# One zero fill of a decode kernel split anew over the 16 DMA engines: 39 small transfers in place of six

## The chip, the cores and the metric

One Trainium2 chip, one of its cores. The metric is the device time of one execution in microseconds (us). Before: a median of 779.5 us over three runs (779.49 to 779.59). In this text "engine" with a number, 0 to 15, is one of the core's 16 DMA engines; TensorE, VectorE (DVE), ScalarE (ACT), GpSimd (POOL) and SyncE (SP) are called by their names.

## The reference

One decode step of a transformer block and its gradients. Sizes: model width D = 448, 16 query heads on 8 key/value heads of width 256, a cache of 32768 positions of which only the last W = 4096 are attended to, a gated feed-forward of width 1792. The core of it:

```python
k = jnp.repeat(k_cache[:, :, Sk - W:, :], rep, axis=1)
v = jnp.repeat(v_cache[:, :, Sk - W:, :], rep, axis=1)
...
h = x + _A_ref(_layernorm(x, axis=-1), A_k_cache, A_v_cache, A_wq, A_wo)
h2 = h + _B_ref(_layernorm(h, axis=-1), B_w_gate, B_w_up, B_w_down)
...
_out, _vjp = jax.vjp(_f, A_x, A_k_cache, A_v_cache, A_wq, A_wo, B_w_gate, B_w_up, B_w_down)
```

The outputs are h2 and the gradients of the eight inputs. The gradients of the two caches (out_2 and out_3) have the caches' full size, 8 x 32768 x 256 in bf16 each. Outside the last 4096 positions they are zero. So for each of the 8 heads and each of the two outputs a region of 28672 x 256 zeros, 14336 KB, has to be written: 16 regions, 224 MB, of the 280.59 MB that the kernel writes in all.

## The kernel before, in words

Computation and zero fills run side by side. The computation loads the last 4096 positions of K and V head by head, makes scores, softmax and the moments that the backward pass needs (L339 to L397), goes through the feed-forward both ways, and in a second loop over the heads (L696) forms the gradients of K and V and stores them through ScalarE's queue (L739). GpSimd forms and stores the weight gradients from about 440 us on. Nothing in the computation reads a fill; the only tie at the end is `fills_done` (L284), where VectorE waits for all fills before it writes one element (L287).

**The fills.** A region is seen as 896 rows of 16384 bytes (ZW = 8192 bf16). The source is a tile of SBUF whose every fourth partition holds zeros: 32 partitions, each read 28 times by a stride of 0 (`rows_of`, L240). One transfer of 896 rows is spread by the chip over all 16 engines, 56 rows each. The first two regions come from the tile `pair` with rows of 32768 bytes (L252). The other 14 come from `home` (`Z_late`), in `fill_late` (L258 to L282), all on SyncE's queue (ZQ). The loop keeps two fills under way: before it issues fill i it waits (L265) until fill i-2 has landed, counted in `zsem[0]` or `zsem[1]`, to which each transfer adds 16. The scheduler moves these waits into the issuing instructions.

**The uneven fill.** One region, number UNEVEN = 3 (the second of the 14), is not spread evenly. Only its first 704 rows go out as one transfer, 44 rows an engine. The other 192 go out as six small transfers, each from a few partitions, so that an engine gets as many rows as the list in L272 says. Each entry is (partitions, first partition, rows from each, queue):

```python
for e, base, rows, queue in ((3, 0, 8, nc.gpsimd), (2, 12, 2, nc.gpsimd), (3, 20, 13, nc.gpsimd), (8, 64, 13, nc.gpsimd), (4, 0, 5, ZQ), (1, 0, 1, ZQ)):
```

A transfer from e partitions runs on e engines. GpSimd's four cover 3 + 2 + 3 + 8 = 16 engines once, with 8, 2, 13 and 13 rows; SyncE's two start again at the first engine, with 5 rows on engines 0 to 3 and one more on engine 0. Counted by engine, 0 gets 8 + 5 + 1 = 14 extra rows, 1 and 2 get 13, 3 gets 2 + 5 = 7, 4 gets 2, and 5 to 15 get 13 each. GpSimd's transfers count in `psem` (64 in all), SyncE's in `zsem[1]`, so that the fill after next waits for SyncE's two as well.

**Order around it.** GpSimd issues its four directly behind the loads of two V tiles (L207), at 131.4 us, and its next instruction is a load of half a K tile (L418) that waits until 235 us. SyncE issues its two between the first late fill and the 704 rows; behind the last fill it has only the waits that end the program (L793).

Of the kernel before, what the change touches and what calls it, by code (L numbers as in the profile page):

```python
# [27 lines left out]
ZW = 16 * KB  # L28
# [7 lines left out]
def kernel(  # L36
        ctx, tc, A_x, A_k_cache, A_v_cache, A_wq, A_wo, B_x, B_w_gate, B_w_up, B_w_down, grad_out,
           out_0, out_1, out_2, out_3, out_4, out_5, out_6, out_7, out_8):
    nc = tc.nc
    LD = nc.scalar  # L40
    ZQ = nc.sync
# [29 lines left out]
    Z_late = home[:]  # L71
# [134 lines left out]
    def load_kv(dst, cache, g, queue=LD):  # L206
        queue.dma_start(out=dst, in_=cache[0, g, Sk - W:, :].rearrange("(p t) d -> p t d", t=T))  # L207
# [32 lines left out]
    def rows_of(src, n):  # L240
        return src[0:128:4].unsqueeze(1).to_broadcast([32, n, src.shape[1]])

    def fill_with(dst, src, sem, group, queue=ZQ):
        fill = queue.dma_start(out=dst, in_=src)
        tc.info.no_tile_sem_insts.add(fill.ins.name)
        tc.add_to_no_dep_group(group, fill.ins)
        tc.keep_in_program_order(fill.then_inc(sem, 16))
# [7 lines left out]
    for g in (5, 6):  # L255
        load_kv(V_of[g], A_v_cache, g, nc.gpsimd)

    def fill_late():  # L258
        zsem = [tc.alloc_semaphore(f"zsem{j}") for j in range(DEEP)]
        psem = tc.alloc_semaphore("psem")  # L260
        due = [0] * DEEP
        for i, reg in enumerate(regions[EARLY:]):
            j = i % DEEP
            if i >= DEEP:
                tc.keep_in_program_order(ZQ.wait_ge(zsem[j], due[j]))  # L265
            n = NZ
            if i + EARLY == UNEVEN:
                odd = reg.rearrange("(r f) -> r f", f=ZW)[22 * 32:]
                reg = reg[0:22 * 32 * ZW]
                n = 22  # L270
                at = 0
                for e, base, rows, queue in ((3, 0, 8, nc.gpsimd), (2, 12, 2, nc.gpsimd), (3, 20, 13, nc.gpsimd), (8, 64, 13, nc.gpsimd), (4, 0, 5, ZQ), (1, 0, 1, ZQ)):  # L272
                    fill_with(odd[at:at + e * rows].rearrange("(e n) f -> e n f", e=e),
                              Z_late[base:base + 4 * e:4].unsqueeze(1).to_broadcast([e, rows, ZW]), zsem[j] if queue is ZQ else psem, "fills", queue)
                    at += e * rows
                    if queue is ZQ:
                        due[j] += 16
            for dst, src in [(reg.rearrange("(p n f) -> p n f", p=32, f=ZW), rows_of(Z_late, n))]:
                fill_with(dst, src, zsem[j], "fills")
                due[j] += 16  # L280
        return zsem, psem, due

    def fills_done(zsem, psem, due):
        tc.keep_in_program_order(nc.vector.wait_ge(psem, 64))  # L284
        for j in range(DEEP):
            tc.keep_in_program_order(nc.vector.wait_ge(zsem[j], due[j]))
        filled = tc.keep_in_program_order(nc.vector.memset(done_t[:], 0.0))  # L287
        tc.declare_fence(filled.ins, group="fills")
# [43 lines left out]
    with tc.tile_pool(name="ps_x", bufs=1, space=bass.MemoryType.PSUM) as ps_x, \  # L332
# [72 lines left out]
        for g in range(G):  # L405
            p_f = p_next
            if g < G - 2:
                p_next = scores(g + 1)
            if g == 1:
                clear_rows()  # L410
                fill_sems = fill_late()
            moments(g, p_f)
            for w, h in NEXT.get(g, ()):
                load_kv((K_of, V_of)[w][h], (A_k_cache, A_v_cache)[w], h)
            if g == G - 4:
                LD.dma_start(out=K_of[G - 1][:, 0:T // 2, :], in_=k_last[:, 0:T // 2, :])
            if g == G - 2:
                nc.gpsimd.dma_start(out=K_of[G - 1][:, T // 2:, :], in_=k_last[:, T // 2:, :])  # L418
                p_next = scores(G - 1)
                LD.dma_start(out=wo_sb[:, JW:], in_=wo_v[:, JW:])  # L420
                LD.dma_start(out=dh_bc[0:1, :], in_=A_x.rearrange("a b d -> (a b) d"))
# [179 lines left out]
    with tc.tile_pool(name="work2", bufs=2) as work2, tc.tile_pool(name="lnw", bufs=1) as lnw, \  # L601
# [94 lines left out]
        for it, g in enumerate((6, 1, 3, 4, 5, 0, 7, 2)):  # L696
# [52 lines left out]
            if it == 6:  # L749
# [16 lines left out]
                nc.vector.tensor_copy(out=dx_bf[:, 384:D], in_=dx_ps[0:1, 384:D])  # L766
                LD.dma_start(out=out_1.rearrange("a b d -> (a b) d"), in_=dx_bf)
        fills_done(*fill_sems)

# [28 lines left out]
```

## Time and profile before

| | |
|---|---|
| median of three runs | 779.5 us |
| the profiled execution: its own time, its span | 779.39 us, 777.6 us |
| written to HBM, read from HBM | 280.59 MB, 49.38 MB |
| SyncE's queue q1, share of 16 engines' time | 75.4% |
| ScalarE's queue q10 | 16.1% |
| GpSimd's queue q0 | 8.0% |
| TensorE, VectorE busy | 58%, 49% |
| last compute instruction ends; last fill's completion | 746.9 us, 775.93 us |

The page has the span in 40 slices with the busy share of the DMA engines in tenths; the view of windows gives that share (1.00 is all 16 engines busy; overlaps of neighbouring packets make it up to 1.01) and the GB/s for any stretch; the waits name who was waited for; the issues name each transfer's queue, size and time to landing. Below them the trace keeps one record for each DMA packet, with queue, start, duration and size. A row of 16384 bytes is one packet, and a transfer's completion is a packet of 4 bytes on each engine.

### The profile page before, as it was taken

The numbers are of one execution on the slowest core, as the hardware profiler recorded it, in microseconds if no ns is written. First come the engines' busy times: TensorE is split into PE (matmuls) and PEld (weight loads), VectorE is DVE, ScalarE is ACT, GpSimd is POOL, SyncE is SP. The second block draws the span as 40 slices with busy tenths as digits, with TensorE's granted clock in tenths as the row PEclk, the third lists the DMA queues.
The fourth block names the chain that finished last, engine by engine and source line by source line (L and its number), as shares of the span: only waits on it lengthen the run. The fifth ranks groups of instructions, "written<-read, shape, count | busy, mean of one in ns | idle before, by whom it ended". The sixth has DMA issues, their size and how long they took to land.

```text
span 777.6 us, 6520 instructions
## 1 busy us (share of the span) xinstructions
PE 450.8 (58%) x2205; PEld 191.2 (25%) x2205; DVE 382.6 (49%) x1132; ACT 198.6 (26%) x309; POOL 196.5 (25%) x113
## 2 busy tenths in 40 slices
PE   1999999796993755231142898532108886830310
PEld 1444444342441322010021233210003332300100
DVE  8168656351570723332369428463104853679520
ACT  1442332334200100000001127332103733540220
POOL 7000001000000010020001157363293938196000
PEclk9999999898896776555555799755558965765555
DMA  9999999999999999999999999999999999999997
GB/s 378 429 422 423 433 438 417 429 429 427 429 430 430 429 430 429 431 431 428 429 432 432 430 429 430 431 429 431 432 432 429 429 429 430 431 429 428 432 431 300
DMA packets 23398, 330.40 MB, mean 425 GB/s; under 512 B 1920, under 2 KB 2181, under 8 KB 4645
## 3 DMA queue, kind: packets, MB, share of 16 engines
q1 hardware_dynamic: 14826, 250.43, 75.4%
q10 hardware_dynamic: 4266, 53.39, 16.1%
q0 software_dynamic: 4272, 26.17, 8.0%
q8 instruction: 17, 0.28, 0.1%
q14 instruction: 17, 0.13, 0.0%
HBM read 49.38 MB, written 280.59 MB: 424 GB/s over the span
## 4 chain that ended last, share of the span: by engine, by line
DVE 16%; PE 15%; DMA 14%; another core or an unknown queue 4%; ACT 2%; issue 1%; DVEq 0%; ACTq 0%
DMA out_dram<-arena 11%; PE d_ps L729 4%; PE rows_ps L322 4%; DVE pair L753 3%; PE tr_ps L319 3%; DVE arena L737 3%; DVE arena L736 3%; DVE arena L551 2%; PE dqb_ps L607 2%; DVE arena L704 1%; DMA arena<-in_B_w_up_dram 1%; PE dqb_ps L613 1%; DMA arena<-in_A_v_cache_dram 1%; ACT arena L734 1%
## 5 line engine op out<-in xcount | busy, mean ns | idle before, releaser
L381 DVE TENSOR_SCALAR arena<-arena,p_f 128x256 bf16<-128x256 bf16 x512 | 109.4, 281 | 29.9 <-PE M_t L385 29.9
L319 PE MATMUL tr_ps<-ident_f,arena 128*128 128x128 f32 x448 | 83.0, 316 | 63.1 <-DMA arena<-in_A_v_cache_dram 41.0
L322 PE MATMUL rows_ps<-arena,vpad 128*16 128x512 bf16 x256 | 87.8, 437 | 11.8 <-DVE arena L704 5.9
L338 ACT COPY arena<-tr_ps 128x1024 bf16<-128x1024 bf16 x64 | 63.5, 1013 | 109.0 <-PE tr_ps L319 105.0
L319 PEld LDWEIGHTS tr_ps<-ident_f,arena 128*128 128x128 f32 x448 | 55.3, 157 | 109.8 <-issue 60.5
L729 PE MATMUL d_ps<-arena 32*128 32x512 bf16 x256 | 48.3, 519 | 55.1 <-DVE arena L737 45.1
L385 PE MATMUL M_t<-arena 128*128 128x512 bf16 x320 | 78.7, 392 | 0.0
L736 DVE CAST arena<-d_ps 128x512 bf16<-128x512 f32 x64 | 44.1, 688 | 49.6 <-PE d_ps L729 48.9
L737 DVE CAST arena<-d_ps 128x512 bf16<-128x512 f32 x64 | 43.5, 680 | 20.9 <-DMA out_dram<-arena 20.9
L733 ACT CAST arena<-d_ps 128x512 bf16<-128x512 f32 x64 | 37.8, 590 | 62.0 <-PE d_ps L729 60.2
L702 ACT COPY arena<-tr_ps 128x1024 bf16<-128x1024 bf16 x32 | 32.6, 1020 | 76.2 <-PE tr_ps L319 57.1
L734 ACT CAST arena<-d_ps 128x512 bf16<-128x512 f32 x64 | 38.2, 596 | 20.5 <-DMA out_dram<-arena 20.5
L385 PEld LDWEIGHTS <-arena 128*128 128x128 bf16 x320 | 30.5, 101 | 38.5 <-issue 10.1
L505 PE MATMUL r_ps<-arena,X2pad 128*2 128x448 bf16 x24 | 10.3, 564 | 49.5 <-DMA arena<-in_B_w_gate_dram 39.1
L324 DVE COPY rows_t<-rows_ps 16x512 f32<-16x512 f32 x8 | 5.4, 679 | 63.4 <-PE rows_ps L322 63.3
L729 PEld LDWEIGHTS <-arena 32*128 32x128 bf16 x256 | 11.1, 96 | 94.1 <-DVE arena L737 60.2
L624 POOL TENSOR_SCALAR arena<-dh_bc,oX_f 128x448 bf16<-128x448 bf16 x18 | 25.1, 1402 | 27.9 <-DMA out_dram<-arena 27.8
L207 POOL DMA_DIRECT2D pair<-in_A_v_cache_dram x2 | 1.3, 632 | 114.7 <-POOLq L253 114.7
L436 POOL DMA_DIRECT2D arena<-in_B_w_gate_dram x4 | 3.1, 773 | 105.9 <-DVE dhn L495 64.5
L704 DVE COPY arena<-tr_ps 128x1024 bf16<-128x1024 bf16 x32 | 22.5, 704 | 14.7 <-PE tr_ps L319 13.4
L322 PEld LDWEIGHTS <-vpad 128*16 128x16 bf16 x256 | 17.4, 90 | 45.0 <-issue 41.0
L385 PE MATMUL M_t<-arena,pair 128*128 128x512 bf16 x128 | 28.0, 379 | 0.0
(257 smaller groups left out, 641.3 us busy)
## 6 DMA issues: line engine op xcount, KB each, us to landing
out_dram<-home SPq DMA_DIRECT2D x13, 14336.0 KB, 78.9
out_dram<-arena ACTq DMA_DIRECT2D x16, 2048.0 KB, 18.6
out_dram<-pair SPq DMA_DIRECT2D x2, 14336.0 KB, 93.6
out_dram<-home SPq DMA_DIRECT2D x1, 11264.0 KB
arena<-in_A_k_cache_dram ACTq DMA_DIRECT2D x4, 2048.0 KB, 20.7
arena<-in_A_k_cache_dram SPq DMA_DIRECT2D x3, 2048.0 KB, 19.6
arena<-in_A_v_cache_dram SPq DMA_DIRECT2D x3, 2048.0 KB
arena<-in_A_v_cache_dram ACTq DMA_DIRECT2D x3, 2048.0 KB, 32.8
```

The lines of the kernel that those rows point to most:

```text
L319: nc.tensor.transpose(tr_ps[:, i, :], X_sb[:, 4 * q + i, :].bitcast(f32), ident_f[:])
L322: nc.tensor.matmul(rows_ps[:], lhsT=pad[:, e, 16 * q:16 * q + 16], rhs=XT.rearrange("p (n e) -> p n e", e=2)[:, :, e], start=(q == 0 and e ...
L338: sT_ps = dots(K_of[g], KT_slot, vpad[g % 2], rows1, ps_c, "cols", lambda q, XT, ps: nc.scalar.copy(out=XT, in_=ps))
L381: nc.vector.tensor_scalar(out=pK[:, i, hh, :], in0=K_sb[:, t, :], scalar1=p_f[:, 8 * i + c, hh:hh + 1], scalar2=None, op0=ALU.mult)
L385: nc.tensor.matmul(M_ps[vh], lhsT=V_sb[:, t, vh * 128:(vh + 1) * 128], rhs=pK[:, i, :, :].rearrange("p h d -> p (h d)"), start=(t == 0), s ...
L702: nc.scalar.copy(out=XT, in_=ps)
L704: nc.vector.tensor_copy(out=XT, in_=ps)
L729: nc.tensor.matmul(d_ps[:, qi].rearrange("p w d -> p (w d)"), lhsT=rm[32 * q:32 * (q + 1), l, :], rhs=Rs[32 * q:32 * (q + 1), :], start=Tr ...
L733: nc.scalar.copy(out=stV[:, t:t + 2, :], in_=d_ps[:, :, 0, :])
L734: nc.scalar.copy(out=stK[:, t:t + 2, :], in_=d_ps[:, :, 1, :])
L736: nc.vector.tensor_copy(out=stV[:, t:t + 2, :], in_=d_ps[:, :, 0, :])
L737: nc.vector.tensor_copy(out=stK[:, t:t + 2, :], in_=d_ps[:, :, 1, :])
```

## The change

The same region is split anew. Its regular transfer shrinks from 704 to 480 rows, 30 an engine. The remaining 416 rows, 26 an engine, go out as 26 transfers on GpSimd's queue and 13 on SyncE's. GpSimd's come in pairs, for m from 2 to 14: one row each from the first m partitions, then two rows each from the other 16 - m. SyncE's 13 no longer stand at the uneven fill: they come behind the last of the 14 fills, one row each from the first k partitions, for k from 14 down to 2. All take the partitions 0, 4, 8 ... 60, where before the last eight were 64, 68 ... 92. `psem` now counts to 416, and the wait for the fill after next counts the 480 rows alone.

```diff
+    def fill_rows(rows, at, e0, k, n, sem, queue):
+        fill_with(rows[at:at + k * n].rearrange("(e n) f -> e n f", e=k),
+                  Z_late[4 * e0:4 * (e0 + k):4].unsqueeze(1).to_broadcast([k, n, ZW]), sem, "fills", queue)
...
-                odd = reg.rearrange("(r f) -> r f", f=ZW)[22 * 32:]
-                reg = reg[0:22 * 32 * ZW]
-                n = 22
+                n = 15
+                single = reg.rearrange("(r f) -> r f", f=ZW)[n * 32:]
+                reg = reg[0:n * 32 * ZW]
                 at = 0
-                for e, base, rows, queue in ((3, 0, 8, nc.gpsimd), (2, 12, 2, nc.gpsimd), (3, 20, 13, nc.gpsimd), (8, 64, 13, nc.gpsimd), (4, 0, 5, ZQ), (1, 0, 1, ZQ)):
-                    fill_with(odd[at:at + e * rows].rearrange("(e n) f -> e n f", e=e),
-                              Z_late[base:base + 4 * e:4].unsqueeze(1).to_broadcast([e, rows, ZW]), zsem[j] if queue is ZQ else psem, "fills", queue)
-                    at += e * rows
-                    if queue is ZQ:
-                        due[j] += 16
+                for m in range(2, 15):
+                    for e0, k, rows in ((0, m, 1), (m, 16 - m, 2)):
+                        fill_rows(single, at, e0, k, rows, psem, nc.gpsimd)
+                        at += k * rows
...
+        for k in range(14, 1, -1):
+            fill_rows(single, at, 0, k, 1, zsem[j], ZQ)
+            due[j] += 16
+            at += k
         return zsem, psem, due
...
-        tc.keep_in_program_order(nc.vector.wait_ge(psem, 64))
+        tc.keep_in_program_order(nc.vector.wait_ge(psem, 26 * 16))
```

Nothing else differs. The order of the instructions on TensorE, VectorE and ScalarE is the same.

## The prediction

> **What bounds the kernel now.** First the page's slices of the span, to see which resource never rests.
>
> ```profile
> DMA  9999999999999999999999999999999999999997
> ...
> q1 hardware_dynamic: 14826, 250.43, 75.4%
> q10 hardware_dynamic: 4266, 53.39, 16.1%
> q0 software_dynamic: 4272, 26.17, 8.0%
> ```
>
> The 16 DMA engines are busy in every slice but the last; the three queues' shares add up to 99.5%. TensorE has 58%. So the span is the DMA work, and the question is how evenly 16 engines finish it. The view of windows over the end (the last two columns are the DMA share and GB/s) shows that:
>
> ```profile
> 746.00:768.00 22.00, 0.00 (x0) 0.00 (x0) 0.88 (x2) 0.71 (x2) 0.00 (x0) 0.50 1.01 434
> 768.00:770.00 2.00, 0.00 (x0) 0.00 (x0) 0.00 (x0) 0.00 (x0) 0.00 (x0) 0.50 0.94 401
> 770.00:772.00 2.00, 0.00 (x0) 0.00 (x0) 0.00 (x0) 0.00 (x0) 0.00 (x0) 0.50 0.67 287
> 772.00:774.00 2.00, 0.00 (x0) 0.00 (x0) 0.00 (x0) 0.00 (x0) 0.00 (x0) 0.50 0.17 74
> 774.00:776.00 2.00, 0.00 (x0) 0.00 (x0) 0.00 (x0) 0.00 (x0) 0.00 (x0) 0.50 0.06 25
> ```
>
> All 16 work until 768; the share then falls as engines run out, to 0.06 = 1/16 from 774 to 776: one engine alone. Compute is over (746.9 us), and the waits (us in total, times, longest) say who waits for that engine, and SyncE's own waits who comes behind:
>
> ```profile
> DVE done_t L287 <- DMA out_dram<-home: 29.6, 1, 29.6
> ```
>
> ```profile
> SPq L793 <- DVE done_t L287: 15.3, 1, 15.3
> ```
>
> The last 16 completions (4-byte packets) of SyncE's queue lie at 768.0, 768.8, 769.6, 770.4, 770.9, 771.5, then seven from 772.1 to 772.6, 774.1, 774.4 and 775.93 us; their mean is 771.9. The span ends 1.67 us after the last, the execution's own time (779.39) 1.79 us after the span.
>
> **Which engine is last.** A packet record names no engine, but on a busy engine a packet starts 3 or 4 ns before its predecessor ends, so records sort into 16 trains. A row of 16384 bytes takes 611 ns, so one every 607 ns; of 15776 such packets after 60 us 14858 took just that. Of the longer ones 889 took up to 700 ns, 12 ns over on average, 10.4 us in all, most of it on one train; it has none while TensorE rests (700 to 720, after 748). I followed this slow train at two places. From 130 to 230 us its GpSimd packets are two V loads of 8 rows and then **2** rows, and its SyncE packets go from 56 rows to 44 with no small transfer between: by front's list this is engine 4, the only one with 2 and none. From 718 to the end no other train has its phase, and it ends at **775.93**. So engine 4 is last although it has 11 rows (6.7 us) less than engines 5 to 15. Engine 3 (2 rows, then 5 of SyncE) carries most of the 309-ns instruction packets of queue q14; where one was clear (at 150.8 us) the row behind it took 1244 ns in place of 611, 0.94 us in all.
>
> **The change part by part.**
>
> *Rows per engine.* Let T be the extra rows beyond an even base of 30. Before: 14 from the 704-row transfer, plus 14 (engine 0), 13 (1, 2), 7 (3), 2 (4), 13 (5 to 15). After: 26 each. The differences are -2 (0), -1 (1, 2), +5 (3), **+10** (4) and -1 (5 to 15), together 0. This takes it that a transfer from k partitions gives k engines one partition each, that GpSimd's go on where the last one stopped and SyncE's start at engine 0. The trains bear it out: the ones with 8 GpSimd rows are those with SyncE's 5. A pair m, 16 - m closes the circle, so each starts at 0.
>
> *Where they lie.* Engine 4 before: 44 + 2 rows by about 220 us. After: 30 regular and 16 of GpSimd's (three transfers of one row skip it, ten of one row and three of two rows use it), again 46; its 10 new rows are all closing ones (k = 14 to 5), behind the last fill. There rows take 611 ns, on this train too: **10 x 0.607 = 6.07 us**. Bounds: 0.607 and 0.640 (its long packets reach 644) give 6.07 to 6.40; I take 6.07, as its last 28 us show.
>
> *Small packets.* Ten more completions at the end: 9 ns long, 6 ns net, +0.06 us. GpSimd's transfers also put a 4-byte packet on an engine for each row that it doesn't get: engine 4 had 38 of GpSimd's in the uneven fill and will have 49 (26 completions, 23 fillers), +0.07 us.
>
> *GpSimd's issue.* The timeline has
>
> ```profile
> 131.40 2.44 POOL L244 DMA_DIRECT2D out_dram<-home  x4
> 235.18 0.57 POOL L418 DMA_DIRECT2D arena<-in_A_k_cache_dram  x1 [101.34 <-PE ok_ps L390]
> ```
>
> Four took 0.60 to 0.67 us each; 26 take 16 to 17.5, until 149. The next instruction waits for TensorE until 235: no cost. If the queue is full, GpSimd stands until it drains: 36 small packets and rows and 4 completions went out from 163 to 199 us, 0.9 us each; 39 and 26 take 58, until some 221, still 14 us before that load. If that cover were gone, the load behind and head 7's scores would start late; compute has 29 us (746.9 to 775.9) less the 10 us an engine needs for the last stores before this shows. The extra turns of q0 also delay ScalarE's loads at 181 and 223 us; the same slack covers them.
>
> *SyncE's issue.* The two small transfers removed had SyncE standing 38.3 and 8.0 us (issues at 71.09 and 109.42) for room in its queue, while the engines had fills to do; nothing is gained. The 13 closing ones stand in the same way behind the last fill (issued at 661.7 us, 0.53 us). Behind them on SyncE are only end waits. An engine would starve only if its rows were all done first, but room comes as the last fill (56 rows, 34 us at least) drains. Cost 0.
>
> *The shorter fill.* L265 now lets fill i = 3 go after 30 rows, not 44. When fill i = 0 lands on the slowest engine the fastest still has 30 x 0.607 = 18 us less its lead; the lead comes from up to 13 rows' difference in GpSimd's share, 7.9 us. No engine idles: 0.
>
> **Sum.** 6.07 + 0.06 + 0.07 = 6.2 us on engine 4, which ends at 782.1; no other passes it (engine 3 ends at 774.4 + 3.0 at most, the rest end at 774.4 less 0.6 at most). Span 783.8, own time 785.6; the profiled execution stood 0.11 under the median, so **785.7 us**, 0.8% slower. Levelling perfectly would give 771.9, but this levels rows, not work.
>
> **The rivals.**
>
> *Not slower: the long packets are the recorder's.* They come while TensorE works, so they might be the profile's own writing. Then, unprofiled, engine 4 ends near 765 before and 772 after, and another engine sets the end: 774.4 before; after it 773.8, or engine 3 up to 777.4 at the worst. The time would be 778.9 to 782.5, most likely 778.9 to 780.5. It decides if over 8 us of the 10.4 vanish without a recorder. Against it: the profiled execution took 779.39, the others 779.49 to 779.59; without engine 4's surplus they should be 1.5 us shorter than it. Chance 0.08 (0.03 faster, 0.05 same).
>
> *Slower still: reading ports.* Engines 8 to 15 now read partitions 32 to 60, beside engines 0 to 7 at 0 to 28. If partitions 32 apart shared a port that one engine fills, 26 rows of an engine would take up to twice 0.607: +15.8 us on one that ended up to 774.4, less 0.6: 789.6, time 793. Against it: the regular fills read 32 partitions at 429 to 434 GB/s, 611 ns a row. Chance 0.03. (The Trainium skill, "SBUF — State Buffer", section "Door 1: The DMA port swizzle", says that partitions p and p + 32 share one of 16 ports, 435 GB/s in all; 32 partitions four apart reach all ports, but an engine that takes two neighbours in turn would have only half of them in use at a time, an estimated 218 GB/s. The trace's 434 disagrees with that as a limit here.)
>
> *Slower still: closing transfers wait for each other.* If each cost an issue of 0.53 us in which its engine idles, engine 4's ten would cost 5.3 more: 791. Against it: SyncE's one-row transfer before follows 5 rows and precedes 44 on engine 0 with only a 9-ns completion between. (The Trainium skill, "DMA: Bandwidth & Descriptors", section "Rules for kernel authors", holds that transfers under 64 KB pay mostly overhead, and its "Anatomy of one DMA" gives about 2.0 us fixed; at that figure ten would cost an estimated 20 us. The trace agrees only for a lone transfer's landing, not for rows queued behind others.) Chance 0.05.
>
> **How the numbers follow.** The forecast has 0.84. Its own range is about 785.7 -1.4 and +0.8: the surplus of engine 4 is from one execution and may shift by 1 us. Upwards I take in a third of the pacing price. Range 784.3 to 787.4. A measurement of this kernel can tell about 0.2% (1.6 us). Faster 0.03, same 0.05, slower 0.92.
>
> **What would show it.** The last completion at 782.1; a DMA share of 0.06 to 0.12 for some 8 us in place of 2; the slow train last, its final 10 rows each followed by a 4-byte completion; most others done by 774; GpSimd issuing until 149 us or standing until 221; compute's end within 5 us of 746.9. Wrong if another train is last, if the 611 ns grow in the closing rows or GpSimd's, if gaps stand between closing rows, or if engine 4 gets another number of rows than 26.

## The result and the profile after

The changed kernel takes a median of 808.6 us over three runs (808.3 to 810.6) against 779.5: the ratio is 1.038, with a 95% interval of 1.0355 to 1.0406. The forecast was 785.7 with 784.3 to 787.4: the direction came out, the size was 29.1 us and not 6.2. The profiled execution took 810.6 us with a span of 808.8.

From the page of the kernel after, the slices of the span (each 20.2 us) and the queues:

```profile
DMA  9999999999999999999999999999999999999962
GB/s 379 431 421 426 430 436 417 428 367 359 369 397 429 428 426 430 433 429 427 430 432 432 431 429 429 432 425 431 433 416 426 429 428 431 428 431 431 382 268 101
...
q1 hardware_dynamic: 14784, 248.12, 72.7%
q10 hardware_dynamic: 4266, 53.39, 15.5%
q0 software_dynamic: 4672, 28.48, 9.0%
```

Read the two rows against each other. The engines are busy in all slices but the last two, yet from the ninth slice to the twelfth (162 to 243 us) they move 359 to 397 GB/s, elsewhere mostly 425 to 433: busy engines that move less. And the last slices fall off more slowly than before. The windows over both places (the stretch; busy time of PE, PEld, DVE, ACT and POOL with counts; granted clock; DMA share; GB/s):

```profile
160.00:200.00 40.00, 27.68 (x159) 12.29 (x160) 10.56 (x52) 15.79 (x20) 0.00 (x0) 0.88 1.00 364
200.00:245.00 45.00, 39.28 (x223) 18.11 (x227) 26.89 (x122) 5.56 (x10) 0.56 (x1) 0.92 1.01 386
...
746.00:768.00 22.00, 5.01 (x33) 0.97 (x32) 10.31 (x16) 9.32 (x17) 0.00 (x0) 0.50 0.94 384
768.00:776.00 8.00, 0.00 (x0) 0.00 (x0) 0.00 (x0) 0.00 (x0) 0.00 (x0) 0.50 0.84 360
776.00:784.00 8.00, 0.00 (x0) 0.00 (x0) 0.00 (x0) 0.00 (x0) 0.00 (x0) 0.50 0.52 221
784.00:792.00 8.00, 0.00 (x0) 0.00 (x0) 0.00 (x0) 0.00 (x0) 0.00 (x0) 0.50 0.50 215
792.00:800.00 8.00, 0.00 (x0) 0.00 (x0) 0.00 (x0) 0.00 (x0) 0.00 (x0) 0.50 0.32 137
800.00:808.00 8.00, 0.00 (x0) 0.00 (x0) 0.06 (x1) 0.00 (x0) 0.00 (x0) 0.50 0.06 27
```

In the kernel before, the first of these stretches reads

```profile
160.00:200.00 40.00, 31.75 (x174) 14.46 (x173) 11.31 (x51) 17.82 (x22) 0.00 (x0) 0.87 1.01 428
```

Two things are to be seen. At 160 to 245 us the share is 1.00 at 364 and 386 GB/s, so the packets themselves have grown long. With 428 as the measure, 64 GB/s are missing for 40 us and 42 for 45 us, 4.45 MB, which is 10.4 us of all engines. The packet records say the same: from 160 to 250 us the rows took 170 us more than their usual 611 ns, summed over the engines (10.6 us for each of 16); before it was 5. And at the end the share stands at **0.52 and 0.50** for 16 us: not one engine is late, eight are.

The trains of packets, followed as in the prediction, agree. Eight end from 773.0 to 776.9 (some had idled, the longest 5.4 us, for ScalarE's last stores), eight from 793.7 to 807.1. The mean of the ends is 786.1, 14.2 later than before, and the last is 21.0 behind the mean, 17.0 more than before. The sum is the 31.2 us by which the two profiled executions differ. The number of closing rows names an engine: the trains that end at 807.1, 801.7 and 798.9 have 10, 13 and 13 of them, and the other late ones 12, 11, 9, 8 and 7. Those are the numbers of engines 4, 0, 1, 2, 3, 5, 6 and 7. So the late ones are **engines 0 to 7**.

The waits of the kernel after (total, times, longest, in us), VectorE's and then SyncE's:

```profile
DVE done_t L293 <- DMA out_dram<-home: 44.9, 1, 44.9
```

```profile
SPq L799 <- DVE done_t L293: 28.6, 1, 28.6
```

VectorE still waits for fills alone. Compute ends at 762.8 us, 15.9 later than before, but 44 us ahead of the last completion. GpSimd's and SyncE's timelines (start, length, what was issued, idle time before and what ended it):

```profile
130.52 14.29 POOL L244 DMA_DIRECT2D out_dram<-home  x26
243.58 0.56 POOL L424 DMA_DIRECT2D arena<-in_A_k_cache_dram  x1 [98.77 <-PE ok_ps L396]
```

```profile
630.65 138.95 SPq L244 DMA_DIRECT2D out_dram<-home  x15
```

GpSimd issued its 26 in 14.3 us without standing. SyncE's line joins two fills and the 13 closing transfers into one stretch until 769.6 us: it stood for room, 47.9 us at the first closing transfer, while the engines had work.

### The profile page after: what moved, and what is told of

It reads as the page before. It is cut to its first block, busy times and chain, and to the rows that moved or that the text cites. A ratio compares the mean times of both kernels' runs of the same rounds, so it can differ in the third digit from the quotient of the medians.

```text
span 808.8 us, 6535 instructions
## 1 busy us (share of the span) xinstructions
PE 442.3 (55%) x2187; PEld 189.8 (23%) x2205; DVE 382.8 (47%) x1132; ACT 198.4 (25%) x309; POOL 206.8 (26%) x135
## 4 chain that ended last, share of the span: by engine, by line
another core or an unknown queue 72%; SPq 14%; PE 5%; DMA 5%; issue 1%; DVE 1%; ACT 0%; DVEq 0%; ACTq 0%
SPq L244 14%; DMA out_dram<-home 5%; PE M_t L391 2%; PE rows_ps L328 1%; PE tr_ps L325 1%; PE q_ps L231 1%; ACT arena L344 0%; PE q_ps L229 0%; PE ok_ps L396 0%; PE cols_ps L333 0%; DVE dh_bc L223 0%; PE nb_ps L353 0%; PE ps L180 0%; PE g_ps L222 0%
## 5 line engine op out<-in xcount | busy, mean ns | idle before, releaser
L328 PE MATMUL rows_ps<-arena,vpad 128*16 128x512 bf16 x256 | 84.3, 422 | 12.5 <-DVE arena L710 6.4
L735 PE MATMUL d_ps<-arena 32*128 32x512 bf16 x256 | 46.3, 499 | 55.7 <-DVE arena L743 45.8
L391 PEld LDWEIGHTS <-arena 128*128 128x128 bf16 x320 | 30.6, 101 | 39.0 <-issue 10.8
L630 POOL TENSOR_SCALAR arena<-arena,xT 128x4096 bf16<-128x4096 bf16 x2 | 21.2, 10617 | 24.7 <-DMA out_dram<-arena 24.7
## 6 DMA issues: line engine op xcount, KB each, us to landing
arena<-in_A_k_cache_dram SPq DMA_DIRECT2D x3, 2048.0 KB, 19.8
```

Source lines behind the costliest of these rows:

```text
L328: nc.tensor.matmul(rows_ps[:], lhsT=pad[:, e, 16 * q:16 * q + 16], rhs=XT.rearrange("p (n e) -> p n e", e=2)[:, :, e], start=(q == 0 and e ...
L391: nc.tensor.matmul(M_ps[vh], lhsT=V_sb[:, t, vh * 128:(vh + 1) * 128], rhs=pK[:, i, :, :].rearrange("p h d -> p (h d)"), start=(t == 0), s ...
L630: nc.gpsimd.tensor_scalar(out=buf[:, off:off + n], in0=src, scalar1=col, scalar2=None, op0=ALU.mult)
L735: nc.tensor.matmul(d_ps[:, qi].rearrange("p w d -> p (w d)"), lhsT=rm[32 * q:32 * (q + 1), l, :], rhs=Rs[32 * q:32 * (q + 1), :], start=Tr ...
```

## The experiments

The theory after the first comparison: engines 8 to 15 read their extra rows from partitions 32 to 60, and these come out of SBUF by the ways that engines 0 to 7 use for the regular fills (the prediction's rival "reading ports"). Against it stood that rows were merely spread unevenly, and, as a second rival, that 39 small transfers cost by their number. Beside the first four kernels before took 779.38 us. In each diff, lines that only follow from the shown ones (the counts that are waited for, the place in the region) are left out; "..." marks these places.

**base32.** The kernel before, with one number changed: the eight engines read from partition 32 on.

```diff
-... (8, 64, 13, nc.gpsimd), ...
+... (8, 32, 13, nc.gpsimd), ...
```

> The kernel before with one number changed: the eight GpSimd pieces of 13 rows (engines 8 to 15) read partitions 32 to 60 instead of 64 to 92. Rows, transfers and queues stay. Partition theory (an engine that reads a partition 32 above another engine's slows that one; in the changed kernel's trace eight trains ended some 25 us late with 26 such rows each, 0.96 us a row): engines 0 to 7 lose 13 x 0.96 = 12.5 us each, engine 4 ends at 788, time 792 us; 787.4 if a row costs only its own 0.607. Transfer theory (the number of small GpSimd transfers and their 4-byte fillers slow the engines) and closing theory (the transfers behind the last fill do it): nothing changed, 779.5 us.

785.24 us (four runs from 784.4 to 787.9), 1.0081 (1.0062 to 1.0100). Windows of base32:

```profile
180.00:200.00 20.00, 7.13 (x36) 3.53 (x36) 0.00 (x0) 6.07 (x6) 0.00 (x0) 0.79 1.00 360
...
768.00:776.00 8.00, 0.00 (x0) 0.00 (x0) 0.00 (x0) 0.00 (x0) 0.00 (x0) 0.50 0.80 342
```

While the 13 rows go out, 360 GB/s at a full share. From 160 to 250 us 95 rows take over 900 ns (before: 5), 83 of SyncE's and 12 of GpSimd's, half of SyncE's 1291 or more, a little over twice 611. From 180 to 200 us the excess is 51 us, or 6.4 on each of eight engines, and eight trains end 779.8 to 781.4 where the others end by 775.5. So a row from the wrong partitions costs another 0.5 us (6.4 / 13). The number written as likeliest, 792, was too high; the bound with one row's 0.607 us for each row, 787.4, was nearer, and also high.

**base96 and base0.** The same number set to 96, and then to 0 (before beside it: 779.43).

> The kernel before with the same eight pieces read from partitions 96 to 124 instead of 64 to 92. Partition theory with a distance of 32 that closes on the same engine (64 and 96 belong together): 779.5 us, no change. If any partition other than the first of an engine's pair costs, engines 8 to 15 lose 13 x 0.96 = 12.5 us and the time is about 787 to 791 us. Transfer and closing theory: 779.5 us.

> The kernel before with the eight pieces of engines 8 to 15 read from partitions 0 to 28, the very ones that engines 0 to 7 read. If partitions 32 to 60 were slow by themselves, or for any engine that doesn't belong there: 779.5 us. If the engines of one group of partitions share one way out, whether the partitions are the same or 32 apart: as with partitions 32 to 60, 785.2 us, with eight trains ending some 8 us after the other eight.

96 gave 779.41 us, 1.0000 (0.9991 to 1.0010); 0 gave 785.25, 1.0077 (1.0062 to 1.0093), with the same dip:

```profile
180.00:200.00 20.00, 7.54 (x40) 3.79 (x40) 0.00 (x0) 6.37 (x7) 0.00 (x0) 0.80 1.01 362
```

So 64 and 96 are alike, 0 and 32 are alike, and partitions 32 to 60 are not slow in themselves: it matters which engines read which half. (The Trainium skill, "SBUF — State Buffer", section "Door 1: The DMA port swizzle (why [64,N] ≈ [32,N])", puts p and p + 32 on one port and p + 64 on another. These three kernels agree with it.)

**even12.** The kernel before, with every engine given the same number of rows, and from the right partitions: the evenness of the change without the rest.

```diff
-... in ((3, 0, 8, nc.gpsimd), (2, 12, 2, nc.gpsimd), (3, 20, 13, nc.gpsimd), (8, 64, 13, nc.gpsimd), (4, 0, 5, ZQ), (1, 0, 1, ZQ)):
+... in ((8, 0, 12, nc.gpsimd), (8, 64, 12, nc.gpsimd)):
...
-nc.vector.wait_ge(psem, 64)
+nc.vector.wait_ge(psem, 32)
```

> The kernel before with the 192 extra rows spread evenly: two GpSimd transfers of 8 x 12 rows (partitions 0 to 28 and 64 to 92), none of SyncE. It tests the prediction's own term alone: engine 4 gets 10 rows more than before, engine 3 five more, all others one or two less. By that term 10 x 0.607 = 6.1 us, 785.6 us, with one train alone at the end. If the slow train's surplus were only the recorder's, 778.9 to 780.5 us. The partition theory adds nothing here.

785.38 us, 1.0076 (1.0059 to 1.0093). The windows of its end:

```profile
768.00:776.00 8.00, 0.00 (x0) 0.00 (x0) 0.00 (x0) 0.00 (x0) 0.00 (x0) 0.50 0.40 170
776.00:784.00 8.00, 0.00 (x0) 0.00 (x0) 0.06 (x1) 0.00 (x0) 0.00 (x0) 0.50 0.04 18
```

One train ends at 781.97, the next at 776.6, the rest by 774.2. This is the state that the prediction described, to 0.1 us at the end of engine 4. The profiled execution (785.40) stands level with the others (785.05 to 785.51), so the long packets of engine 4 are not the recorder's.

**gp_ports.** The change, with the reading taken away: GpSimd's transfers cut at engine 8, and the pieces for engines 8 to 15 read from partition 64 on, 36 transfers in place of 26.

```diff
-for m in range(2, 15):
-    for e0, k, rows in ((0, m, 1), (m, 16 - m, 2)):
-        fill_rows(single, at, e0, k, rows, psem, nc.gpsimd)
+for m in (2, 3, 4, 5, 6, 8, 8, 8, 10, 11, 12, 13, 14):
+    for e0, e1, rows in ((0, m, 1), (m, 16, 2)):
+        for lo, hi, first in ((e0, min(e1, 8), e0), (max(e0, 8), e1, max(e0, 8) + 8)):
+            if lo < hi:
+                fill_rows(single, at, first, hi - lo, rows, psem, nc.gpsimd)
...
```

> The changed kernel with GpSimd's pieces cut at engine 8, so that engines 8 to 15 read partitions 64 to 92: 36 GpSimd transfers instead of 26, rows per engine the same but for one row between engines 7 and 8. The 13 closing transfers stay, 21 of their rows still read 32 above another engine's. Partition theory: the stretch of 360 to 400 GB/s between 160 and 245 us goes, 785.7 us of the prediction plus two closing rows against engine 4, about 787.6 us. Transfer theory: 36 transfers cost more than 26, 808 us or more. Closing theory: the early loss goes (about 10 us of all engines) and the late eight trains stay, about 798 us.

793.89 us, 1.0186 (1.0171 to 1.0201): none of the three. From its page (slices of 19.8 us):

```profile
GB/s 378 428 423 427 432 431 424 422 420 386 379 375 416 424 426 429 432 430 431 426 430 433 431 430 432 429 431 429 432 427 430 427 427 423 432 430 429 432 412 204
```

Slices 10 to 12 still dip, to 375. If each of GpSimd's pieces ran on the engines that the code means, none of them would read from the wrong half. So the pieces ran elsewhere. The trains of the kernel after had the clue: some carry rows of both transfers of a pair ("row, completion, row, row, completion"), which is impossible if the second goes on where the first stopped. The second theory: **a GpSimd transfer of single rows always starts at engine 0, and doesn't move the place where the next one starts; only those that read a partition several times go round.** By it the extra rows of engines 0 to 15 are 40, 40, 38, 36, 34, 32, 30, 28, 24, 22, 20, 18, 16, 14, 12 and 12, not 26 each. (The sum: engine e gets one row from each m above e, one closing row from each k above e, and the 104 turns of the two-row transfers go 6.5 times around, so 14 rows for engines 0 to 7 and 12 for the others.)

The next four kernels tell this apart (before beside them: 779.56).

**half.** The change, but each single row goes out as two half rows, so that these transfers too read a partition more than once. The engines that read and the partitions stay those of the code.

```diff
-fill_rows(single, at, e0, k, rows, psem, nc.gpsimd)
+if rows == 1:
+    half_rows(single, at, e0, k, psem, nc.gpsimd)
...
+def half_rows(rows, at, e0, k, sem, queue):
+    fill_with(rows[at:at + k].rearrange("e (h f) -> e h f", h=2),
+              Z_late[4 * e0:4 * (e0 + k):4, 0:ZW // 2].unsqueeze(1).to_broadcast([k, 2, ZW // 2]), sem, "fills", queue)
```

> The changed kernel with GpSimd's 13 one-row transfers written as two half rows of 8 KB from each partition, a form with a repeat like that of its other 13. Bytes, partitions, queue and number of transfers stay. Two-cause theory, formed from the trains of the changed kernel: (1) a GpSimd transfer of single rows starts at engine 0 each time and doesn't move on the place where the next begins, so engines 0 to 7 got 28 to 40 rows and engines 8 to 15 12 to 24; (2) rows read from partitions 32 to 60 hold up engines 0 to 7. With the repeat the first cause goes, all engines get 26, and the second stays: engine 4 at 782 plus up to 26 x 0.607 = 15.8 us, time about 801, some 7 us under the changed kernel. If ports alone did it: 808. If the number of transfers did it: 808.

800.08 us, 1.0264 (1.0249 to 1.0279): 8.5 us of the change's 29.1 go with the form of the transfer alone.

**half_ports.** Both cures: half rows, and the pieces cut as in gp_ports.

> The run before with half rows and with the pieces cut at engine 8, so that engines 8 to 15 read partitions 64 to 92; 36 GpSimd transfers, 13 closing ones. Two-cause theory: both causes are gone but for 21 closing rows, two of them (engine 12's) against engine 4: 785.7 to 788 us, and no stretch under 415 GB/s between 130 and 250 us. If small transfers by themselves cost: 794 us (as with whole single rows) or more. In the tail every train shows its number by its count of closing rows.

786.30 us, 1.0088 (1.0071 to 1.0105). Windows of half, then of half_ports:

```profile
180.00:200.00 20.00, 10.36 (x50) 5.10 (x48) 1.35 (x2) 7.60 (x8) 0.00 (x0) 0.78 1.00 371
200.00:245.00 45.00, 38.66 (x211) 16.84 (x214) 25.58 (x120) 4.14 (x9) 0.56 (x1) 0.88 1.00 379
...
776.00:784.00 8.00, 0.00 (x0) 0.00 (x0) 0.00 (x0) 0.00 (x0) 0.00 (x0) 0.50 0.52 221
```

```profile
180.00:200.00 20.00, 15.63 (x67) 7.60 (x65) 1.83 (x5) 10.07 (x13) 0.00 (x0) 0.73 1.02 430
200.00:245.00 45.00, 33.88 (x196) 14.60 (x198) 25.05 (x117) 2.37 (x6) 0.56 (x1) 0.88 1.01 426
...
776.00:784.00 8.00, 0.00 (x0) 0.00 (x0) 0.06 (x1) 0.00 (x0) 0.00 (x0) 0.50 0.21 88
```

The dip from 160 to 245 us is in half (the excess of its packets is 147 us) and gone in half_ports. The difference of the two, **13.8 us**, is the price of the reading. Half's trains end like those of after, eight at 776.3 and eight from 787.7 to 796.3, though by the second theory each engine has the same number of rows there.

**ones12.** The second cause alone: even12 with its two transfers written as 24 of single rows, from the right partitions by the code's idea of the engines.

```diff
-... in ((8, 0, 12, nc.gpsimd), (8, 64, 12, nc.gpsimd)):
+... in ((8, 0, 1, nc.gpsimd), (8, 64, 1, nc.gpsimd)) * 12:
...
```

> The even version of two transfers of 8 x 12 rows (785.4 us) with its 192 rows in 24 transfers of 8 single rows, in turn from partitions 0 to 28 and 64 to 92. If a transfer of k partitions always takes the next k engines, as the prediction had it: 785.4 us. By the two-cause theory all 24 run on engines 0 to 7, which get 24 rows each and engines 8 to 15 none: engine 4 has 12 more than in the even version, 7.3 us, 792.7 us, up to 7 us more where its rows from 64 to 92 have to share, and eight trains end some 14 us before the other eight.

793.02 us, 1.0174 (1.0159 to 1.0189). Its windows:

```profile
768.00:776.00 8.00, 0.00 (x0) 0.00 (x0) 0.00 (x0) 0.00 (x0) 0.00 (x0) 0.50 0.67 287
776.00:784.00 8.00, 0.00 (x0) 0.00 (x0) 0.00 (x0) 0.00 (x0) 0.00 (x0) 0.50 0.30 127
784.00:792.00 8.00, 0.00 (x0) 0.00 (x0) 0.06 (x1) 0.00 (x0) 0.00 (x0) 0.50 0.04 18
```

Eight trains end by 774.0, eight from 778 to 789.6, as if engines 0 to 7 had 24 rows and the others none: 12 rows more than in even12 are 7.3 us, and 7.6 were measured. (The Trainium skill, "DMA: Bandwidth & Descriptors", section "Why a DMA increments its semaphore by 16 and not by 1", lets GpSimd's transfers go round from a cursor, and has some direct copies spread over all 16 engines by their partitions. It doesn't say which; here those of single rows behave as the second kind would, which for 16 partitions or fewer begins at engine 0.)

This trace also shows who pays for the reading here. If engines 0 to 7 run all 24 transfers, half of these take their rows from the partitions of engines 8 to 15. From 160 to 250 us 81 of SyncE's rows take over 900 ns (4 in even12), but only one of GpSimd's. The nearest packets of GpSimd before and after such a long row on its train, looked for within three places, are 53 times 4-byte ones and 2 times rows; around SyncE's rows of usual length, from 150 to 200 us, they are 791 and 501. So the long rows lie on the engines that got no rows from GpSimd, 8 to 15, whose partitions are read by others. These had time to spare, and the end doesn't show it.

**many26.** Number alone: 26 even GpSimd transfers of 8 partitions with two rows each, from the right partitions, no closing ones, beside even12's two of twelve rows.

```diff
-for m in range(2, 15):
-    for e0, k, rows in ((0, m, 1), (m, 16 - m, 2)):
-        fill_rows(single, at, e0, k, rows, psem, nc.gpsimd)
+for m in range(13):
+    for e0 in (0, 16):
+        fill_rows(single, at, e0, 8, 2, psem, nc.gpsimd)
...
-for k in range(14, 1, -1):
-    fill_rows(single, at, 0, k, 1, zsem[j], ZQ)
...
```

> The changed kernel with all 416 rows in 26 GpSimd transfers of 8 partitions x 2 rows, in turn from partitions 0 to 28 and 64 to 92, and no closing transfers: every engine gets 26 rows from its own partitions. Two-cause theory: the same time as with two transfers of 8 x 12, 785.4 us. If the number of GpSimd transfers costs anything, more than that: a tenth of the changed kernel's loss would be 3 us.

786.0 us, 1.0084 (1.0069 to 1.0099), 0.6 more than even12 with its two, of which 0.2 is the difference of the two befores; the intervals of the ratios overlap. So their number costs next to nothing, for transfers of this size (256 KB).

**level.** The kernel before, with the same kind of list, set by the ends of the trains: 20 regular rows from each partition, and fewer extra ones for engines 3 and 4 than for the others (before beside it: 779.43).

```diff
-... in ((3, 0, 8, nc.gpsimd), (2, 12, 2, nc.gpsimd), (3, 20, 13, nc.gpsimd), (8, 64, 13, nc.gpsimd), (4, 0, 5, ZQ), (1, 0, 1, ZQ)):
+... in ((3, 0, 7, nc.gpsimd), (2, 12, 2, nc.gpsimd), (3, 20, 19, nc.gpsimd), (8, 64, 18, nc.gpsimd), (4, 0, 6, ZQ), *((1, 0, 1, ZQ),) * 6):
...
```

> A version meant to beat both: 20 regular rows from each partition instead of 22, and the 256 extra rows spread by the ends that the even versions showed (engine 4 at 782, one train at 776.6, one at 774.2, the rest 768.5 to 772). Against an even 16, engine 4 gets 14 less, engine 3 8 less, engines 1 and 2 3 less, engine 0 3 more, 5 to 7 3 more, 8 to 15 2 more. If rows simply add up at 0.607 us, engine 4 ends at 773.5 and no train after 774: 777 us. If engine 3 isn't the train at 776.6, or 1 or 2 not the one at 774.2, up to 1.8 us later: 779 us. If more rows on GpSimd's queue hold up the load behind them and with it the last stores: 780 us or more.

778.89 us, 0.9990 (0.9982 to 0.9999), eleven runs from 777.0 to 780.1: far under the changed kernel, but only 0.1% under before, which lies inside what such a measurement can tell. It came out at the second of the three numbers written down, 779, and not at the 777 of rows that simply add up. In the profile its trains end from 767.7 to 774.9, the last 2.8 us behind their mean of 772.1; before it was 4.0.

## Why the prediction was wrong

The sum by measured steps, in medians: evenness 5.9 (even12), 24 transfers more 0.6 (many26), closing rows and cut pieces 0.3 (half_ports less many26), reading 13.8 (half less half_ports), assignment 8.5 (after less half). Together 29.1, as they must, since each step starts where another ends; the two steps under 1 us lie within the intervals of the ratios.

- **Engine 4 last by its ten rows: right, as far as its row count went.** Put alone (even12), the 6.2 us came out at 5.9, and the last completion at 781.97 where 782.1 was written. Engine 4 is the last in after, too, but for other reasons as well: 22.3 of the 29.1 us are the reading and the assignment, which the sum put at nothing. The part that was right is a fifth of what was measured.
- **"A pair m, 16 - m closes the circle, so each starts at 0": the step that failed.** It was inferred from transfers of several rows (8, 2, 13 and 13), and carried over to transfers of one row, of which the trace of before has none on GpSimd's queue. Half and ones12 show that these behave otherwise, by 8.5 and 7.6 us. Engine 4 gets 34 extra rows by the second theory, not 26, engines 0 and 1 get 40.
- **The rival "reading ports", at 0.03: the second failure, and the larger one (13.8 us; its own price was 7.3 over the forecast).** The evidence against it was that 32 partitions four apart are read at 429 to 434 GB/s. But this says nothing of 16 engines on 16 partitions, if in a regular fill each engine has the two partitions p and p + 32 to itself. Base0, base32 and base96 show that the halves differ; that the regular fill is dealt out in that way is the inference that fits them. The rival had the right mechanism, but was priced for engines 8 to 15 alone: the long rows are those of SyncE's fills more often than GpSimd's (83 and 12 of the 95 in base32), so engines 0 to 7 pay as well, and engine 4 among them was the last already.
- **Closing transfers wait for each other (0.05): no.** In the tail a closing row and its completion follow every 0.61 us. (The 2.0 us that the prediction quotes there from the Trainium skill is that page's figure for GpSimd's path, and the rule beside it is on transfers under 64 KB; engine 4's ten closing transfers are SyncE's and have 80 to 224 KB.) One sign of being wrong did show: from 757 to 766 us 24 rows, all of SyncE's queue, took over 900 ns, up to 1485, 15 us in all; the closing transfers, too, read partitions 32 to 52 for engines 8 to 13. **The long packets are the recorder's (0.08): no**, by even12.
- **Small packets, SyncE's standing, GpSimd's issue: right, as far as can be seen.** A closing row with its completion takes 613 ns, 6 more than a row, as written; the fillers' 0.07 us can't be told apart. 26 issues took 14.3 us (16 to 17.5 written), and it ended at 144.8. SyncE's standing cost nothing to see.
- **Compute's end within 5 us of 746.9: wrong, and hidden.** The cover of GpSimd's next load held: GpSimd was free from 144.8 on and waited 98.8 us for TensorE. It was TensorE that came late: its waits for loads of K and V, in the stretches from 130 us to that load, before and after, grew by 7.7 and 1.0 us.

```profile
PE tr_ps L319 <- DMA arena<-in_A_k_cache_dram: 7.5, 1, 7.5
PE ok_ps L390 <- DMA arena<-in_A_v_cache_dram: 4.0, 1, 4.0
...
PE tr_ps L325 <- DMA arena<-in_A_k_cache_dram: 15.2, 1, 15.2
PE ok_ps L396 <- DMA arena<-in_A_v_cache_dram: 5.0, 1, 5.0
```

GpSimd's load was issued at 243.6 instead of 235.2, and compute ended 15.9 us later. The last stores then came after some of engines 8 to 15 had nothing left, which idled up to 5.4 us. Engines 0 to 7 set the end, so it cost nothing here. In half_ports compute ended at 767.5, and from 762 to 768 us the DMA share fell to between 0.29 and 0.41, as engines ran dry before the last stores. The slow train worked on without a gap and ended last, at 783.0, with its share of those stores, 5 us behind the others.

Open: which of two engines on one way out pays in general. In ones12 it is the one whose own partitions are read, and in half and after engines 0 to 7, whose partitions are read, end late; but in after 88 of GpSimd's rows took over 900 ns as well, and there and in base32 the trains are not to be told apart through the dip. Open, too, is the whole of the 8.5 us: the train with ten closing rows ends 10.8 us later in after than in half, and its 8 rows more are 4.9. An estimate for the rest: if each engine has the two partitions p and p + 32 to itself, then by the second theory 225 of GpSimd's rows in after are read from another engine's two, and 187 in half. The excess of the packets (170 and 147 us, less the 5 of before) is 0.73 and 0.76 us for each of these. For the two partitions of engine 4 the counts are 30 and 24, and six more at 0.73 are 4.4 us. No run tries the wrong partitions of the right half alone, so this isn't shown. Why engine 4's packets are long while TensorE works wasn't tried.

## What to carry to other kernels

Equal row counts are no equal finish: give the rows by the measured ends of the engines, and check in the packet trains that each engine got the rows that the code meant for it. What a small transfer does is to be read from one of its own form (single or repeated rows, the same partitions); a neighbour form may be dealt out otherwise. A full DMA share with falling GB/s means long packets, and the partitions that are read are the first place to look.

## What the runs showed of the hardware

- GpSimd's transfers of one row for each of up to 14 partitions behave as if they started at engine 0 each time; those of repeated rows take turns (793.0 against 785.4 us for the same rows, ones12 and even12; 808.6 against 800.1, after and half).
- With partitions four apart, 0 to 28 and 32 to 60 behave as if they were read through the same ways, and 64 to 92 and 96 to 124 through others: rows of 611 ns grow, mostly to some 1000 to 1320 ns, when engines of both halves read from one (base0 and base32, +5.8 us for 13 rows on eight engines).
- 24 more small transfers in GpSimd's queue, beside engines that are busy anyway, cost 0.6 us in all, if anything (many26 against even12).
- Where GpSimd's rows for engines 0 to 7 come from the partitions of engines 8 to 15, it is SyncE's rows on engines 8 to 15 that grow long (81 over 900 ns, one of GpSimd's; ones12).
